# Weights ahead of later activations at the start, a different order in the first row tile, and a bank and an add moved

## The chip, the cores and the metric

The program runs on one core of one Trainium2 chip. The metric is device time in microseconds (us), of which the time before the change was 933.08 us in the median of its first three runs. Beside the device time each run lists its *span*, from the first to the last instruction of the core. The span is 1.7 to 3.5 us shorter than the device time and scatters less, so where a few tenths matter I compare spans. I also use the mean granted clock of TensorE that each run lists.

## The reference, cut to what matters

```python
xn = layernorm(x)                                     # x: 2048 x 640
s  = attention(xn, k_cache, v_cache, wq) @ wo         # 32 heads, window of 512 keys
g  = silu((silu(xn @ w_gate) * (xn @ w_up)) @ w_down) # w_gate, w_up: 640 x 1536
out = x + s * g
```

The kernel does the feed-forward part first, 512 rows at a time in four blocks, and then attention over pairs of heads. The change touches only the first 20 us (loads, layer norm and the first gate and up products) and the last 10 us (the final multiply and add of the last row tiles).

## The kernel before: what the change and the argument touch

Loads. A load has a queue, SP's or ACT's, and the order of issue on a queue is the order below. `load_gu(q)` brings one quarter of the columns of `w_gate` and of `w_up`, 480 KB each.

```python
def load_x(t):                              # one row tile: 128 rows of x, 160 KB
    ...
    if t < 2:
        for r, eng in ((lo, nc.sync), (hi, nc.scalar)):    # half on each queue
            eng.dma_start(out=x_t[t][r, :], ...)
    else:
        nc.sync.dma_start(out=x_t[t][:], ...)
...
for t in range(4):
    load_x(t)
load_gu(0, nc.scalar)                       # w_gate on SP's queue, w_up on ACT's
load_gu(1)
```

The first block goes row tile by row tile, because its rows arrive that way. For every row tile the layer norm takes statistics and a normalization on VectorE (and a square root on ACT), five transposes on TensorE into the PSUM tile `tp`, and a copy of `tp` to `xnT`, on ACT (`ready`; for row tile 0 VectorE takes two of the five chunks). `first[f]` are PSUM tiles for the first three chunks of 128 hidden columns; index 0 is gate and 1 is up. `keep_warm(n)` issues n dummy matmuls on zeros.

```python
first = {f: [sc[:, s, :] for s in range(2)] for f, sc in ((0, sc_tile()), (1, sc_tile()))}
first[2] = [mm[:, s, :] for mm in (mm_tile(),) for s in range(2)]
tp = psum.tile([P, 2, 1024], bf, name="tp", tag="mm")     # two buffers with tag "mm"
...
ln_stats(1, lambda: ln_apply(0))       # tile 0's normalization between the halves of tile 1's statistics
ready(0)
keep_warm(2)
for t in range(4):
    for f in range(3):
        if f == 2 and t < 3:
            if t < 2:
                ln_stats(t + 2, lambda: ln_apply(t + 1))
            else:
                ln_apply(t + 1)
            ready(t + 1)
        for s in range(2):             # gate, then up, of the same chunk
            hidden_mm(first[f][s][:, rows], s, f, rows)   # a group: 5 matmuls of 128 columns
        if t == 3:
            hidden_gate(0, f, *first[f])                  # Silu on ACT, then multiply on VectorE
...
def ffn_hidden(b, f):                  # every later chunk, 512 columns at once
    gu = sc_tile()
```

At the end, for each of the last row tiles, VectorE multiplies the projection in PSUM by `g2` (`s_f`) and then VectorE (`V`) or POOL (`G`) adds the accumulated sum (`ob`). The very last tile is done in two halves, both on VectorE.

```python
for qt in range(4):
    store(2)
    wo_last(3, qt, G if qt else V)
```

The softmax here doesn't subtract the row's maximum and nothing guards it: scores larger than these inputs give would overflow.

## Time and profile before

| | before |
|---|---|
| device time, median of the first 3 runs | 933.08 us |
| span of the profiled run | 931.3 us |
| TensorE busy | 99% |
| first gate matmul of row tile 0 | 8.83 us |
| first 512-column matmul (fourth chunk) | 19.23 us |
| last matmul's end to the end of the span | 5.34 us |

The two points in time in the middle of the table split the kernel into three stretches. The first is the wait for data, the second is the four row tiles of the first block, and all of the rest is one stretch in which TensorE hardly ever stops.

From the page of the kernel before: the first line of the part on busy time, and the shares by engine of the chain of work that ended last.

```profile
PE 921.0 (99%) x8008; PEld 580.2 (62%) x8024; DVE 579.9 (62%) x845; ACT 476.2 (51%) x849; POOL 66.6 (7%) x58
...
PE 98%; DMA 1%; DVE 1%; ACT 0%; SPq 0%; issue 0%; DVEq 0%
```

TensorE (PE) is the limit. Only 10.3 us of the span lie outside its work, and nearly all of that is at the two ends.

The timeline of the kernel before, at its start. Columns: start in us, duration in us, engine, line, operation, output and inputs, count, and in brackets how long the engine had been idle and for what.

```profile
3.34 1.00 SPq L190 DMA_DIRECT2D wg_sb<-in_B_w_gate_dram  x2
...
6.19 0.59 PE L213 MATMUL sc<-zero_t 128*128 128x512 bf16 x2
...
6.90 0.29 DVE L321 COPY xnT<-tp 128x256 bf16<-128x256 bf16 x1 [0.75 <-ACT xnT L319]
...
8.83 0.45 PE L269 MATMUL sc<-xnT,wg_sb 128*128 128x128 bf16 x5 [2.04 <-DMA wg_sb<-in_B_w_gate_dram]
...
9.46 0.74 PE L269 MATMUL sc<-xnT,wg_sb 128*128 128x128 bf16 x5
...
14.76 0.44 PE L269 MATMUL sc<-xnT,wg_sb 128*128 128x128 bf16 x5 [0.22 <-ACT xnT L319]
...
19.23 1.24 PE L269 MATMUL sc<-xnT,wg_sb 128*128 128x512 bf16 x4 [0.30 <-DVE hT L277]
```

The normalized row tile 0 is in `xnT` at 7.19 us, but the weights are not there: issued fifth on the queue, at 3.34, they let TensorE start at 8.83. Then a group of five matmuls takes 0.74 us where it takes 0.44 later (0.53 against 0.28 from one group's start to the next). Two more waits follow, for ACT's copy and, before the fourth chunk, for VectorE to release a PSUM buffer.

The same kernel by windows of one microsecond. The last three columns are the granted clock, the DMA share and GB/s.

```profile
core 0: us, PE busy (x) PEld busy (x) DVE busy (x) ACT busy (x) POOL busy (x), PEclk, DMA share, GB/s
...
8.00:9.00 1.00, 0.17 (x3) 0.17 (x4) 0.96 (x4) 0.00 (x0) 0.00 (x0) 1.00 1.10 329
9.00:10.00 1.00, 1.00 (x16) 1.00 (x14) 0.14 (x1) 0.00 (x0) 0.00 (x0) 0.66 1.10 325
10.00:11.00 1.00, 1.00 (x12) 1.00 (x11) 0.00 (x0) 0.00 (x0) 0.00 (x0) 0.50 1.10 328
...
13.00:14.00 1.00, 1.00 (x22) 1.00 (x20) 0.48 (x2) 0.00 (x0) 0.00 (x0) 1.00 1.11 333
```

TensorE is "1.00 busy" at 10 us and at 13 us, yet it completes 12 matmuls in the one and 22 in the other. The granted clock is the reason: by the trace's records it is half from 9.32 to 12.74 us. (The records begin at 5.91 us, with the first full-speed mark. Before that mark the PEclk column shows 1.00 because nothing is recorded; the 512-column dummies there follow each other at 0.43 us, against 0.216 later.)

The timeline of the kernel before, at its end.

```profile
924.12 3.04 POOL L541 TENSOR_TENSOR ob<-s_f,sacc 128x640 bf16<-128x640 f32 x2 [3.09 <-DVE s_f L538]
...
925.40 0.57 PE L495 MATMUL mm<-wo_p,OT_b 128*128 128x320 bf16 x3
...
925.72 1.78 DVE L536 TENSOR_TENSOR ob<-s_f,sacc 128x320 bf16<-128x320 f32 x1
927.43 0.48 DVE L535 TENSOR_TENSOR s_f<-mm,g_76 128x320 f32<-128x320 f32 x1
927.94 0.49 DVE L536 TENSOR_TENSOR ob<-s_f,sacc 128x320 bf16<-128x320 f32 x1
```

VectorE's add of half a tile takes 1.78 us at 925.72 and 0.49 us at 927.94. The long one runs while POOL adds two tiles of its own, until 927.16.

### The profile page before, as it was taken

To read this page: it belongs to the slowest core of one execution; us is meant where nothing else is said; L and a number is where in the kernel's file an instruction comes from. 1 tells how busy PE (TensorE), PEld (TensorE's weight loads), DVE (VectorE), ACT (ScalarE), POOL (GpSimd) and SP (SyncE) were. 2 spreads that over 40 slices of the span, in tenths; PEclk is the share of its full clock that TensorE was granted. 3 is DMA by queue.
4 is the path that set the end of the run, shared out by engine and by line. 5 is a ranking of instruction groups with operands and counts; after the bars stand their busy time and mean duration, and the time that the engine had idled before them with its cause. 6 is when DMAs were issued, how large, how long until landed. Compare 5 with 4: busy or idle time off the path is not lost.

```text
span 931.3 us, 18790 instructions
## 1 busy us (share of the span) xinstructions
PE 921.0 (99%) x8008; PEld 580.2 (62%) x8024; DVE 579.9 (62%) x845; ACT 476.2 (51%) x849; POOL 66.6 (7%) x58
## 2 busy tenths in 40 slices
PE   8999999999999999999999999999999999999997
PEld 5455556574757575757575757565666666666675
DVE  5433321377676767676766767676767676767656
ACT  3222222566565655555555555555555555656561
POOL 0000000000000000000000000000000000003976
PEclk9999999999999999999999999999999999999999
DMA  9312510044434434343434252525262616162523
GB/s 297 71 27 61 113 24 11 1 78 86 81 83 74 89 71 91 72 92 67 97 60 104 55 108 53 110 48 116 41 122 35 128 35 128 35 139 64 146 60 107
DMA packets 240100, 76.34 MB, mean 82 GB/s; under 512 B 221072, under 2 KB 240016, under 8 KB 240016
## 3 DMA queue, kind: packets, MB, share of 16 engines
q1 hardware_dynamic: 239200, 74.48, 37.8%
q8 instruction: 63, 1.03, 0.5%
q10 hardware_dynamic: 816, 0.66, 0.3%
q14 instruction: 21, 0.17, 0.1%
HBM read 39.45 MB, written 2.62 MB: 45 GB/s over the span
## 4 chain that ended last, share of the span: by engine, by line
PE 98%; DMA 1%; DVE 1%; ACT 0%; SPq 0%; issue 0%; DVEq 0%
PE sc L495 22%; PE mm L412 22%; PE mm L448 18%; PE sc L426 18%; PE sc L269 11%; PE mm L291 6%; PE sc L448 1%; DMA wg_sb<-in_B_w_gate_dram 1%; PE mm L304 0%; DVE ob L536 0%; SPq L184 0%; ACT xnT L319 0%; PE mm L426 0%; ACT L325 0%; PE mm L269 0%
## 5 line engine op out<-in xcount | busy, mean ns | idle before, releaser
L430 ACT ACTIVATE p_t<-sc 128x1024 bf16<-128x1024 f32 x254 | 253.1, 1023 | 136.4 <-PE sc L426 136.4
L417 DVE TENSOR_REDUCE qT<-mm 128x512 bf16<-128x1024 f32 x189 | 231.3, 1224 | 104.0 <-PE mm L412 101.6
L465 ACT ACTIVATE O_b<-mm,r 128x192 bf16<-128x192 f32 x484 | 164.5, 422 | 175.2 <-DVE r L454 96.5
L412 PE MATMUL mm<-xnT,wq_p 64*128 64x512 bf16 x1890 | 235.0, 376 | 0.0
L495 PE MATMUL sc<-wo_p,OT_b 128*128 128x320 bf16 x1482 | 223.4, 299 | 0.0
L510 DVE TENSOR_TENSOR sacc<-sacc,sc 128x640 f32<-128x640 f32 x216 | 176.7, 821 | 60.9 <-PE sc L495 60.9
L426 PE MATMUL sc<-qT,khat 64*128 64x512 bf16 x1524 | 195.5, 376 | 0.0
L448 PE MATMUL mm<-V_p,p_t 128*128 128x193 bf16 x1984 | 185.8, 246 | 0.0
L448 PEld LDWEIGHTS <-p_t 128*128 128x128 bf16 x2048 | 173.0, 97 | 14.9 <-issue 7.0
L495 PEld LDWEIGHTS <-OT_b 128*128 128x128 bf16 x1488 | 143.5, 98 | 47.3
L412 PEld LDWEIGHTS <-wq_p 64*128 64x128 bf16 x1890 | 90.7, 94 | 112.4 <-issue 4.2
L426 PEld LDWEIGHTS <-khat 64*128 64x128 bf16 x1536 | 74.7, 94 | 91.0
L277 DVE TENSOR_TENSOR hT<-sc,sg 128x512 bf16<-128x512 f32 x47 | 32.4, 690 | 86.2 <-ACT sg L276 86.2
L513 POOL TENSOR_TENSOR sacc<-sacc,g_76 128x640 f32<-128x640 f32 x16 | 22.1, 1402 | 757.8 <-ACT O_b L465 757.8
L454 DVE RECIPROCAL r<-mm 128x4 f32<-128x4 f32 x124 | 22.7, 183 | 73.1 <-PE mm L448 68.9
L276 ACT ACTIVATE sg<-sc 128x512 bf16<-128x512 f32 x47 | 28.0, 597 | 75.2 <-PE sc L269 72.1
L269 PE MATMUL sc<-xnT,wg_sb 128*128 128x512 bf16 (+1 forms) x252 | 59.4, 357 | 3.5 <-DMA wg_sb<-in_B_w_gate_dram 2.0
L269 PE MATMUL sc<-xnT,wu_sb 128*128 128x512 bf16 (+1 forms) x264 | 59.8, 357 | 0.1
L291 PE MATMUL mm<-wd_sb,hT 128*128 128x320 bf16 x384 | 56.6, 299 | 0.0
L291 PEld LDWEIGHTS <-hT 128*128 128x128 bf16 x384 | 37.6, 98 | 18.9
L269 PEld LDWEIGHTS <-wg_sb 128*128 128x128 bf16 x285 | 26.7, 101 | 26.3 <-DMA wg_sb<-in_B_w_gate_dram 2.5
L269 PEld LDWEIGHTS <-wu_sb 128*128 128x128 bf16 x285 | 26.5, 100 | 26.5
(63 smaller groups left out, 249.1 us busy)
## 6 DMA issues: line engine op xcount, KB each, us to landing
wo_p<-in_A_wo_dram SPq DMA_DIRECT2D x16, 480.0 KB, 4.3
K_p<-in_A_k_cache_dram SPq DMA_DIRECT2D x32, 192.0 KB, 3.4
V_p<-in_A_v_cache_dram SPq DMA_DIRECT2D x32, 192.0 KB, 3.1
wq_p<-in_A_wq_dram SPq DMA_DIRECT2D x64, 80.0 KB, 3.1
wq_p<-in_A_wq_dram SPq DMA_DIRECT2D x16, 160.0 KB, 3.2
x_r<-in_A_x_dram SPq DMA_DIRECT2D x16, 160.0 KB, 3.6
x_t<-in_A_x_dram SPq DMA_DIRECT2D x14, 160.0 KB, 3.0
wg_sb<-in_B_w_gate_dram SPq DMA_DIRECT2D x4, 480.0 KB, 6.6
```

The costliest lines, as they stand in the source:

```text
L269: nc.tensor.matmul(out, w_sb[:, c, f * P : (f + 1) * P], xnT[:, c, qc], start=(c == 0), stop=(c == NC - 1),)
L276: nc.scalar.activation(sg[:], g, ACT.Silu)
L277: nc.vector.tensor_tensor(hTs[b][:, f, :], u, sg[:], ALU.mult)
L291: nc.tensor.matmul(dn[:, 0:HD], hTs[b][:, f, ti * P : (ti + 1) * P], wd_sb[:, f, cols], start=(f == 0), stop=(f == NF - 1),)
L412: nc.tensor.matmul(q_ps[:, h, :], pairs[pr]["wq"][r, c, j * P : (j + 1) * P], xnT[r, c, b * 512 : (b + 1) * 512], start=(c == 0), stop=(c ...
L417: nc.vector.reduce_sum(qTs[i][:, j, :], q_ps[:, :, :].rearrange("p h n -> p n h"), axis=AX.X)
L426: nc.tensor.matmul(sc[:, h, :], khat[r, j, ks], qT[r, j, :], start=(j == 0), stop=(j == 2))
L430: nc.scalar.activation(p_t[:, :, :], sc[:, :, :], ACT.Exp, scale=scale)
L448: nc.tensor.matmul(acc[:, k, h * 256 : h * 256 + Dh + 1], Ps[i][kc][:, h, qt * P : (qt + 1) * P], V_p[:, kc, h, 0 : Dh + 1], start=(kc == ...
L465: nc.scalar.activation(O_b[:, qt, h, :], a_k[:, h, 0:Dh], ACT.Copy, scale=r[:, k, h, :])
L495: nc.tensor.matmul(ps, OTs[i][:, 3 * qt + j, :], pairs[i // NB]["wo"][:, j, n * HD : (n + 1) * HD], start=(first and j == 0), stop=(end an ...
L510: nc.vector.tensor_tensor(s_t, s_t, sc[:, :, 0:HD], ALU.add)
```

## The change

Its intent: bring the first weight quarter before row tiles 2 and 3 of x, since row tile 0 needs it first; let row tile 0 do all gate groups before the up groups, since `w_gate` lands ahead of `w_up`; fill the shorter wait with four dummies; put the fourth chunk into the buffer of the transposes, which is free early; and let POOL add only one of the last tiles.

```diff
         def load_x(t, eng=nc.sync):
-            if t < 2:
+            if t == 0:
                 for r, eng in ((lo, nc.sync), (hi, nc.scalar)):
...
-        for t in range(4):
-            load_x(t)
+        load_x(0)
+        load_x(1, nc.scalar)
         load_gu(0, nc.scalar)
+        load_x(2)
+        load_x(3)
         load_gu(1)
...
-            gu = sc_tile()
+            gu = mm_tile() if (b, f) == (0, 3) else sc_tile()
...
+        tp = psum.tile([P, 2, 1024], bf, name="tp", tag="mm")
         first[2] = [mm[:, s, :] for mm in (mm_tile(),) for s in range(2)]
-        tp = psum.tile([P, 2, 1024], bf, name="tp", tag="mm")
...
-        keep_warm(2)
+        keep_warm(4)
         for t in range(4):
-            for f in range(3):
-                if f == 2 and t < 3:
+            order = [(f, s) for s in range(2) for f in range(3)]
+            for k, (f, s) in enumerate(order if t == 0 else sorted(order)):
+                if k == 4 and t < 3:
                     ...                          # statistics, normalization, transposes of tile t+1
-                for s in range(2):
-                    hidden_mm(first[f][s][:, rows], s, f, rows)
+                hidden_mm(first[f][s][:, rows], s, f, rows)
...
-        wo_last(3, qt, G if qt else V)
+        wo_last(3, qt, V if qt else G)
```

More of the change, by code (lines that the diff above doesn't have):

```diff
@@ L178, with load_x @@
         x_t, ln, xns = {}, {}, {}
-        def load_x(t):
+        def load_x(t, eng=nc.sync):
             x_t[t] = lnx.tile([P, D], bf, name="x_t")
-            if t < 2:
+            if t == 0:
                 for r, eng in ((lo, nc.sync), (hi, nc.scalar)):
@@ L185, in load_x @@
             else:
-                nc.sync.dma_start(out=x_t[t][:], in_=x2[t * P : (t + 1) * P, :])
+                eng.dma_start(out=x_t[t][:], in_=x2[t * P : (t + 1) * P, :])
         def load_gu(q, eng=nc.sync):
@@ L340 @@
                     ready(t + 1)
-                for s in range(2):
-                    hidden_mm(first[f][s][:, rows], s, f, rows)
-                if t == 3:
+                hidden_mm(first[f][s][:, rows], s, f, rows)
+                if t == 3 and s == 1:
                     hidden_gate(0, f, *first[f])
```

## The prediction

> What bounds it. TensorE is busy 99% of the 931.3 us span and is 98% of the chain that ended last (page). Of the 10.3 us without a matmul, 5.3 us are the tail after the last one (ends 925.97) and about 4.0 us lie in the first 19.3 us (timeline), so only edges can gain. The middle has DMA far from full and is not touched. The change edits both edges.
>
> Start, before (timeline, chain of waits). xnT of row tile 0 is ready at 7.19 us, but w_gate's first quarter, fifth on the SP queue (issued 3.34), lands 5.44 us later; TensorE idles 2.04 us, to 8.83. Then the granted clock is 0.5 from about 9.3 to 12.6 (windows: 0.66, 0.50, 0.50, 0.63): five 128-column matmuls take 0.53 us instead of 0.28. That costs about 3.3 x 0.5 = 1.65 us. I read it as the Trainium skill, "TensorE: Matmul & The Clock Gate", Part 1: a free-running activity window of about 3.4 us gates the clock to half after too little work; the 3.3 us here agree. Row tiles 2 and 3 wait 0.22 us each for ACT's xnT copy, and the fourth chunk waits 0.30 us for VectorE to free its bank (at 19.23).
>
> Start, after.
> - w_gate's quarter is issued second on SP, about 1.4 instead of 3.34. Bytes ahead of its end are about 1.1 MB less; with the slow first 2 us of the queues I estimate landing at 6.9 to 7.3, w_up's at 7.2 to 7.7 (6.8 before).
> - x tile 1 goes whole to ACT's queue, landing about 4.2, no later than before: VectorE's order (stats of tile 1, then apply of tile 0) doesn't slip. x tile 2 slips from before 7.1 to about 7.5, so xn of tile 1 comes about 8.5 instead of 8.14.
> - Gate columns first need w_up 0.56 us later than before. Four warming matmuls (4 x 0.22) end at 7.05, so no idle window.
> - Row tile 0 starts at 7.1 to 7.4 (minus 1.5 us). Clock stays full (minus 1.65). Because the work is faster, tile 1 now waits for ACT's copy and xn, 0.3 to 0.7 us (plus 0.5). Tiles 2 and 3 follow at the 2.34 us period seen before.
> - Fourth chunk in the transposes' bank: minus 0.30.
> Sum: first 512-column matmul at about 16.3 instead of 19.23: minus 2.9. Everything later is TensorE-bound and shifts with it.
>
> Tail. Before, the last half tile's VectorE add takes 1.78 us instead of 0.49, because POOL adds the two tiles before it until 927.2 (Trainium skill, "SBUF — State Buffer", SBUF: two separate sides: a GpSimd op and a VectorE op with two SBUF inputs exclude each other; the add ends 0.34 us after POOL, which agrees). After, POOL adds only the first tile (about 922.5 to 924.05), VectorE the next two, 0.82 each. Adding VectorE's queue from 922.8: first add held until 924.05, ends 924.72, then 0.82+0.82+0.48+0.49+0.43+0.49 gives 928.3, against 928.43. The contention becomes queueing: about minus 0.1.
>
> Predicted: 933.1 - 2.9 - 0.1 = 930.1; I take 930.3 for DMA luck. Range 929.4 to 931.8. Within 2%: 98%.
>
> What would show it: first gate matmul at about 7.2; PEclk full from 6 us on; no wait for VectorE before the fourth chunk; first 512-column matmul near 16.3; last matmul to end of span still about 5.2 us; VectorE adds of the last tiles 0.82, 0.49 instead of 1.78.
>
> What would make it wrong: the two weight quarters contending so that gate lands after 8; x tile 2 landing after 8, holding tile 1; the clock window falling otherwise in either kernel (run-to-run about 1.2 us in the before times); x tile 1 landing after 4.4, delaying tile 0.

## The result

| | before | after |
|---|---|---|
| device time, median (6 runs each) | 933.22 us | 931.0 us |
| span of the profiled run | 931.3 | 928.8 |
| first gate matmul of row tile 0 | 8.83 | 7.66 |
| first 512-column matmul | 19.23 | 17.05 |
| from the one to the other | 10.40 | 9.39 |
| last matmul's end to the end of the span | 5.34 | 5.04 |

The ratio of the times is 0.9976, with a 95% interval of 0.9963 to 0.9989. It is the mean time of the changed kernel's fast runs over the mean of the other's fast runs of the same rounds, so it is not quite the ratio of the medians. The change gains 2.2 us of device time, where I predicted 2.8 (933.1 to 930.3).

The page of the changed kernel, the same two lines.

```profile
PE 920.7 (99%) x8026; PEld 578.7 (62%) x8026; DVE 579.7 (62%) x846; ACT 476.2 (51%) x849; POOL 65.1 (7%) x57
...
PE 98%; DMA 1%; DVE 1%; ACT 0%; issue 0%; SPq 0%; DVEq 0%
```

Nothing is to be seen at this scale: a gain of 2.2 us in 931 does not show in shares. The start, in the timeline of the changed kernel:

```profile
1.38 0.80 SPq L190 DMA_DIRECT2D wg_sb<-in_B_w_gate_dram  x1
...
6.05 1.03 PE L215 MATMUL sc<-zero_t 128*128 128x512 bf16 x4
...
7.66 0.73 PE L271 MATMUL sc<-xnT,wg_sb 128*128 128x128 bf16 x10 [0.58 <-DMA wg_sb<-in_B_w_gate_dram]
...
8.37 0.49 DVE L225 BATCH_NORM_STATS2 stats<-x_t 128x6 f32<-128x320 bf16 x1 [1.32 <-DMA x_t<-in_A_x_dram]
...
8.96 0.45 DVE L248 TENSOR_SCALAR xn<-x_t,mv,rstd 128x640 bf16<-128x640 bf16 x1
...
9.47 0.45 PE L259 MATMUL tp<-ident,xn 128*128 128x128 bf16 x5 [0.52 <-DVE xn L248]
...
10.70 0.44 PE L271 MATMUL sc<-xnT,wg_sb 128*128 128x128 bf16 x5 [0.22 <-ACT xnT L321]
...
17.05 1.24 PE L271 MATMUL mm<-xnT,wg_sb 128*128 128x512 bf16 x5
```

The weights come earlier and TensorE starts 1.17 us sooner. But a new wait has come: VectorE waits 1.32 us for the x of row tile 2, which now lies behind the weights on SP's queue, and the normalization of row tile 1 stands behind it in VectorE's order. The transposes of tile 1 wait for that at 9.47, and row tile 1 starts only at 10.70. The wait before the 512-column matmul is gone.

By windows, the changed kernel:

```profile
9.00:10.00 1.00, 0.53 (x10) 0.54 (x11) 0.96 (x4) 0.04 (x1) 0.00 (x0) 1.00 1.09 328
10.00:11.00 1.00, 0.78 (x15) 0.66 (x13) 0.54 (x3) 0.85 (x2) 0.00 (x0) 1.00 1.11 336
...
13.00:14.00 1.00, 0.96 (x18) 0.96 (x18) 0.61 (x2) 0.98 (x2) 0.00 (x0) 1.00 1.10 330
```

The granted clock stays at 1.00. And the end:

```profile
920.35 1.54 POOL L543 TENSOR_TENSOR ob<-s_f,sacc 128x640 bf16<-128x640 f32 x1 [1.50 <-DVE s_f L540]
...
921.50 1.08 DVE L543 TENSOR_TENSOR ob<-s_f,sacc 128x640 bf16<-128x640 f32 x1
...
923.34 0.83 DVE L543 TENSOR_TENSOR ob<-s_f,sacc 128x640 bf16<-128x640 f32 x1
...
925.53 0.49 DVE L538 TENSOR_TENSOR ob<-s_f,sacc 128x320 bf16<-128x320 f32 x1
```

VectorE's 1.78 us add is gone; one add of a whole tile is still held a little by POOL (1.08 instead of 0.83 us). VectorE ends 2.23 us after the last matmul (923.79), against 2.46 before.

The difference of the two profiled spans, 2.47 us, splits so: 1.17 (start of row tile 0) + 1.01 (row tiles) + 0.29 (the rest). What lies in the 1.01 was the question for the experiments: how much is the clock, how much the bank, and what the new wait takes back.

### The profile page after: what moved, and what is told of

It is laid out like the page before. It is cut to its first block, busy times and chain, and to the rows that moved or that the text cites. A ratio compares the mean times of both kernels' runs of the same rounds, so it can differ in the third digit from the quotient of the medians.

```text
span 928.8 us, 18808 instructions
## 1 busy us (share of the span) xinstructions
PE 920.7 (99%) x8026; PEld 578.7 (62%) x8026; DVE 579.7 (62%) x846; ACT 476.2 (51%) x849; POOL 65.1 (7%) x57
## 4 chain that ended last, share of the span: by engine, by line
PE 98%; DMA 1%; DVE 1%; ACT 0%; issue 0%; SPq 0%; DVEq 0%
PE sc L497 22%; PE mm L414 22%; PE mm L450 18%; PE sc L428 18%; PE sc L271 10%; PE mm L293 6%; DMA x_t<-in_A_x_dram 1%; PE sc L450 1%; PE mm L306 0%; PE mm L271 0%; ACT xnT L321 0%; DVE s_f L540 0%; PE mm L428 0%; ACT L327 0%; DVE ob L538 0%
```

## The experiments

### The wait filled with dummies, nothing else

```diff
-        keep_warm(2)
+        keep_warm(11)          # in the kernel before
```

> The kernel before with one edit: 11 instead of 2 dummy matmuls ahead of row tile 0, so that TensorE has work (9 more x 0.216 us) until about 8.5 us, where w_gate's first quarter lands at 8.8. Theory (an idle window of about 2 us makes the clock fall to half from 9.3 to 12.6 us): the granted clock stays 1.00 after 6 us, row tile 0 still starts at 8.8, and the first 512-column matmul comes about 1.6 us earlier minus one exposed wait for ACT's copy of tile 1 (0.4): at 18.0 instead of 19.23. Time down 1.2 us, and the runs closer together than the 1.9 us of before. Rival (the clock falls for another reason, such as its phase or the start of dense real data): still about 0.5 between 9 and 13 us, first 512-column matmul at 19.2, time the same.

The granted clock stayed at 1.00. The gate weights landed late in this execution (first gate matmul at 9.36), but from there to the first 512-column matmul it took 9.15 us instead of 10.40. The windows of this kernel:

```profile
9.00:10.00 1.00, 0.96 (x14) 0.64 (x13) 0.66 (x3) 0.00 (x0) 0.00 (x0) 1.00 1.10 329
10.00:11.00 1.00, 1.00 (x22) 1.00 (x20) 0.00 (x0) 0.03 (x1) 0.00 (x0) 1.00 1.10 328
```

Twenty-two matmuls between 10 and 11 us, where the kernel before made 12, and a difference of 1.25 us in the row tiles, net of the copy wait that a fall hides. That fits idle time as what takes the clock away, but this one profile does not show it, since the kernel before also has executions without a fall; the shares of all profiles, in the next section, are the evidence. Yet the time did not change: ratio 0.9998 (0.9986 to 1.0011), 932.36 us against 932.32. The expectation of 1.2 us was wrong, and the list of runs shows why. The nine runs of the kernel before in these rounds are of two sorts: three have a span of 931.5 to 931.9 us and a mean clock of 0.997 or 0.998, and six have 929.9 to 930.5 and 0.999 or 1.0. By this, the clock fell at the start in a third of the runs only. I call these bad draws and the others good ones. The dummies' five runs had spans of 930.0 to 930.7, all with a clock of 0.999 or 1.0: they show no bad draw and gain nothing on a good one. (They may cost a little on a good one, since eleven dummies end at about 9.3 us even when the weights land sooner. That is argued, not shown.)

### The kernel before, twice more

> The kernel before once more, unedited, for another profile of its start. Theory (the clock falls only when the phase of the 3.4 us windows puts most of the idle time into one of them, so in some executions and not in others): w_gate lands at 8.8 to 9.5; with a fall the row tiles 0 and 1 take 5.9 us from the first gate matmul to row tile 2, without one 4.7, and the span is 931.5 to 931.9 or 929.9 to 930.5. Rival: always a fall, span 931 or more.

> The same as the run above, another draw: a fall and 5.9 us, or none and 4.7 us.

Both draws came. The first has no fall: first gate matmul at 8.72, first 512-column matmul at 17.87, which is 9.15 us, and a span of 930.0.

```profile
8.72 0.45 PE L269 MATMUL sc<-xnT,wg_sb 128*128 128x128 bf16 x5 [1.73 <-DMA wg_sb<-in_B_w_gate_dram]
...
17.87 1.24 PE L269 MATMUL sc<-xnT,wg_sb 128*128 128x512 bf16 x5 [0.29 <-DMA wg_sb<-in_B_w_gate_dram]
```

(The wait in the last bracket is put down to a load, but that quarter had landed by about 10 us; VectorE's first multiplication, from 17.13 to 17.8, is what frees the buffer. The releasers are inferred, and the same wait of 0.29 has VectorE as its releaser in the next fence.) The second has a fall, from 10.6 us on: 9.50, then 19.90, which is 10.40 us, and a span of 932.0.

```profile
9.50 0.45 PE L269 MATMUL sc<-xnT,wg_sb 128*128 128x128 bf16 x5 [2.10 <-DMA wg_sb<-in_B_w_gate_dram]
...
19.90 0.81 PE L269 MATMUL sc<-xnT,wg_sb 128*128 128x512 bf16 x3 [0.29 <-DVE hT L277]
```

So the same program takes 9.15 or 10.40 us for the same work, as the clock has it. Over the three sets of rounds the kernel before was run 27 times: 17 runs with spans of 931.2 to 933.0 us and a mean clock of 0.998 or less, 10 with 929.9 to 930.5 and 0.999 or more. (The sets ran on three chips: 3 of 9 runs fell on the first, 7 of 9 on each of the others. The good draws agree across chips, with means of 930.2 to 930.4, so spans can be compared between sets when like draws are.) The profile that I predicted from is of the first sort too. (The mean clock alone is not enough: it also counts the last few microseconds of the span, when TensorE has stopped and the clock can fall again, so a run without a fall at the start can show 0.998, as the profiled one of "the normalization of tile 1 ahead" below does. The two sorts are 0.7 us apart in span.)

When does it fall? The trace records the changes of the clock, and they lie on a grid of windows of 3.41 us. In each of the 14 profiles I took the share of the window after the first full-speed mark in which TensorE was busy. The four profiles with a fall had 34, 38, 39 and 40%. The ten without had 48, 49, 57 and more. The windows at the end of the span, where TensorE stops, agree and narrow it: one with 43% was not followed by a half clock, three with 37 to 38% were. The windows are found from the records; that the share of one window decides is inferred from these figures.

What differs between executions is two things. The first is the length of the gap, which the landing of `w_gate` ends: in the first of the two above it is 1.73 us, and wherever a window of 3.41 us is laid over that trace, TensorE has at least 49%, so by these figures it would not have fallen at any phase. In the four that fell it was 2.04 to 2.24 us. That also fits the spans: a bad draw is 1.6 us longer than a good one on average, 0.3 more than the fall itself costs. The second is the phase of the windows relative to the program (the first mark lies between 4.6 and 7.2 us). In the five profiles with this load order and two dummies the gap lay whole in one window. The one profile in which a window's edge cut it in two is the next one. So how much of the draw is phase and how much landing is not shown.

### The load order alone

```diff
-        for t in range(4):
-            load_x(t)
+        load_x(0)
+        load_x(1, nc.scalar)
         load_gu(0, nc.scalar)
+        load_x(2)
+        load_x(3)              # in the kernel before; row order, dummies, banks and tail as before
```

> The kernel before with the new load order alone (w_gate and w_up ahead of x tiles 2 and 3, x tile 1 whole on ACT's queue); row order, 2 dummies, banks and tail as before. Theory: w_gate lands at 7.6, w_up at 8.3, x tile 2 at 8.35 as in the profile after, so row tile 0 starts at 7.65, waits about 0.4 for w_up, and row tile 1 is held by x tile 2 (its stats stand ahead of the normalization of tile 1 on VectorE) and starts at 10.7 as after. If the clock stays full: first 512-column matmul at 17.5 (17.05 plus the bank wait), minus 1.7 us; if the idle time (about 1.2 + 0.4 + 0.6 us) makes the clock fall, at 18.5 to 19. This tells what the gate-first row order and the two more dummies add to the load order: theory nothing but the safety of the clock.

The gate weights landed only at 8.85 in the profiled execution, and the x of tile 2 at 9.64 (expected 7.6 and 8.35): the landing of one and the same load order varies by more than a microsecond. In the trace's records of DMA packets one of the 16 engines finished its part of `w_up` at 8.83 us, the other 15 by 7.26; a load has landed when the slowest has. The row tiles took 9.90 us, which is the 9.15 of a full clock, plus 0.28 for `w_up` between the first gate and the first up group, plus 0.46 for the x of tile 2. The clock did not fall (48% busy in the window), by luck of the phase: the gap of 2.37 us was cut at 8.15, and a window that held it whole would have had 26%. The five spans were 929.3 to 931.2, mean 930.16: no better than a good draw of the kernel before, 930.2. By itself the load order is meant to bring the weights sooner; in this profile they landed no sooner (8.85 against 8.79), and it adds the two waits. By their clock at most one of the five runs can have fallen (one shows 0.998, the others more), against three of nine of the kernel before; that is too few to show that bad draws get rarer. The time is not resolved from before (ratio 0.9996, 0.9983 to 1.0008).

### The bank alone, and the tail alone

```diff
+        tp = psum.tile([P, 2, 1024], bf, name="tp", tag="mm")
         first[2] = [mm[:, s, :] for mm in (mm_tile(),) for s in range(2)]
-        tp = psum.tile([P, 2, 1024], bf, name="tp", tag="mm")
...
-            gu = sc_tile()
+            gu = mm_tile() if (b, f) == (0, 3) else sc_tile()
```

> The kernel before with the bank swap alone (transposes' bank taken first, fourth chunk in that bank). Theory: the 0.30 us wait for VectorE before the fourth chunk goes, first 512-column matmul about 0.45 us after the same point of row tile 3 (2.13 us from tile 3's first matmul to it becomes 1.67); nothing before it moves: start of row tile 0 at 8.8, the half clock from about 9.3 on again (a second look at whether the clock falls in another execution). Rival: the wait only moves to the fifth chunk, whose bank is freed by the same VectorE multiplication; then no gain at the sixth chunk. Time down 0.3 to 0.5 us, inside the noise of this kernel.

```profile
9.15 0.45 PE L269 MATMUL sc<-xnT,wg_sb 128*128 128x128 bf16 x5 [2.24 <-DMA wg_sb<-in_B_w_gate_dram]
...
19.09 1.24 PE L269 MATMUL mm<-xnT,wg_sb 128*128 128x512 bf16 x4
```

The clock fell here, and the row tiles took 9.94 us where 10.40 is the figure with a fall: 0.46 less. The stretch from the first 512-column matmul to the end of the span was 912.09 us, against 912.08 in the kernel before, so the wait did not move to the sixth chunk. (In the timeline that wait reads 0.30; from one group's start to the next it is 0.46, because the idle time is counted only from the modelled end of the last matmul.) The times don't resolve it: 1.0006, 0.9993 to 1.0018. By their spans (930.9 to 931.5) and a clock of 0.998 all five runs fell, against three of nine of the kernel before beside them; why so many is not known. Bad draw against bad draw, the mean span is 931.2 against 931.7, which agrees with the 0.46.

```diff
-        wo_last(3, qt, G if qt else V)
+        wo_last(3, qt, V if qt else G)     # in the kernel before
```

> The kernel before with the last row tiles' adds swapped alone (first on POOL, next two on VectorE). Theory from the two profiles: end of the last matmul to the end of the span falls from 5.33 to about 5.0 us, VectorE's last add 2.23 us after the last matmul's end instead of 2.46, since VectorE's own queue is then the limit; time down 0.2 to 0.3 us. Rival (my prediction): minus 0.1 or nothing. The start is that of before, with a half clock from about 9.3 us if the clock falls in every execution.

```profile
923.18 1.54 POOL L541 TENSOR_TENSOR ob<-s_f,sacc 128x640 bf16<-128x640 f32 x1 [1.50 <-DVE s_f L538]
...
928.36 0.49 DVE L536 TENSOR_TENSOR ob<-s_f,sacc 128x320 bf16<-128x320 f32 x1
```

From the last matmul's end to the end of the span it took 5.11 us, where the kernel before took 5.33 to 5.35 in its three profiles; VectorE ended 2.23 us after the last matmul. The gain is 0.22 to 0.24 us, more than my 0.1, and far below the 1.3 us by which the one add had been stretched: what POOL no longer holds up, VectorE now has to do itself. The times (1.0001, 0.9987 to 1.0014) do not resolve 0.2 us; by their spans three of the five runs fell.

### The changed kernel with the old order in row tile 0

```diff
-            for k, (f, s) in enumerate(order if t == 0 else sorted(order)):
+            for k, (f, s) in enumerate(sorted(order)):        # in the changed kernel
```

> The changed kernel with the row order of before in row tile 0 (gate and up alternating). Theory (row tile 1 is held by x tile 2, so time lost in tile 0 on w_up comes out of a later wait): row tile 0 waits 0.3 to 0.5 us for w_up's quarter after its first gate group, row tile 1 still starts at 10.7 plus or minus the luck of the landings, first 512-column matmul at 17.0, span the same as after within 0.3. Rival (the gate-first order earns what it was meant to): 0.4 us later.

The weights landed at 8.2 and the x of tile 2 at 9.0, a bad draw, but from the first gate to the first 512-column matmul it took 9.48 us, as in the two profiles of the changed kernel (9.39 and 9.49). The five spans were 928.6 to 929.5, mean 928.9; the changed kernel's eleven had a mean of 929.1. The gate-first order earns nothing here, because row tile 1 waits for the x of tile 2 either way.

### The changed kernel without its dummies

```diff
-        keep_warm(4)               # in the changed kernel
```

> The changed kernel without its 4 dummy matmuls before row tile 0. Theory: nothing of the time is theirs as such; TensorE idles from about 6.2 to 7.65 instead of from 7.05, and the clock only falls if a window of 3.4 us has less than about 40 to 49% work (40, 38 and 34% in the three profiles that fell, 49% in the one with the new loads that did not). Expect 50 to 56% here: no fall in the profile, row tile 1 at 10.7, first 512-column matmul at 17.0, spans 929 like after, with one or two of the runs about 1.3 us longer with a mean clock of 0.998 or less. Rival (the four dummies are what keeps the clock): a fall in most runs, spans 930.3 or more.

The profile had no fall (57% busy in its window), row tile 1 at 10.68, the first 512-column matmul at 17.02 and a span of 928.8, as in the changed kernel. Four of the five runs had 928.7 to 929.1; one had 930.6, with a clock of 0.998. The dummies have no worth of their own, but without them a bad draw seems to happen; with them none of eleven runs has such a span (two show a clock of 0.998, with 929.1 and 929.3 like the rest). One run in five is thin evidence. The traces say more: wherever a window of 3.41 us is laid over the start of the changed kernel, TensorE has at least 67% in one profile and 80% in the other; without the dummies the least is 44%, close to the 40% of a fall.

### The normalization of tile 1 ahead of the statistics of tile 2

```diff
-                    if t < 2:
+                    if t == 0:                 # in the changed kernel
+                        ln_apply(1)
+                        ln_stats(2)
+                    elif t < 2:
                         ln_stats(t + 2, lambda: ln_apply(t + 1))
```

> The changed kernel with one edit: on VectorE the normalization of row tile 1 stands ahead of the statistics of tile 2, instead of between their halves. Theory (in the profile after, row tile 1 is held because tile 2's x lands at 8.35 us behind w_gate's quarter, and VectorE waits for it 1.32 us with the normalization of tile 1 behind it): xn of tile 1 at about 7.7, transposed at 8.8 after the fourth group instead of 9.47, row tile 1 starts at 10.0 instead of 10.7, first 512-column matmul at 16.4 instead of 17.05; span down about 0.7 us from the 929.1 mean of after. Rival (row tile 1 is held by something else: ACT's copy, w_up, TensorE's own work): row tile 1 within 0.2 us of 10.7, span the same.

Row tile 1 started at 9.88, the first 512-column matmul at 16.23. The lines of this kernel's timeline:

```profile
7.59 0.45 DVE L248 TENSOR_SCALAR xn<-x_t,mv,rstd 128x640 bf16<-128x640 bf16 x1
...
8.66 0.44 PE L259 MATMUL tp<-ident,xn 128*128 128x128 bf16 x5
...
9.88 0.44 PE L271 MATMUL sc<-xnT,wg_sb 128*128 128x128 bf16 x5 [0.22 <-ACT xnT L321]
```

The normalization now runs at 7.59 instead of 8.96, and the transposes follow the fourth group without a wait. Row tile 0 started at 7.54, so the row tiles took 8.69 us instead of 9.39 to 9.49: 0.7 to 0.8 us, as the theory has it. Four of the five spans were 927.8 to 928.0, one was 929.3; the device time was 929.72 us, ratio to before 0.9964 (0.995 to 0.9978). So the new wait was the x of tile 2, through VectorE's order. (The 929.3 has a clock of 1.0, so it is no fall.)

### The x of tile 2 on ACT's queue, w_up behind w_gate on SP's

```diff
         load_x(1, nc.scalar)
-        load_gu(0, nc.scalar)
-        load_x(2)
+        load_x(2, nc.scalar)           # in the changed kernel
+        load_gu(0)
         load_x(3)
```

> The changed kernel with one edit: x tile 2 goes to ACT's queue behind tile 1, and w_up's quarter to SP's queue behind w_gate's. Theory (w_gate's quarter lands at 7.6, later than the 6.9 to 7.3 that I predicted, because w_up's quarter shares the 16 engines with it from the other queue; and x tile 2 waits behind both): w_gate lands at about 6.7, w_up at 7.8, x tile 2 before 6; row tile 0 starts at 7.1, tile 1 at 9.5, first 512-column matmul at 15.9 instead of 17.05; span down 1.1 us. Rival (the slow first packets of a queue and single late engines set the landing, not the sharing): w_gate still lands after 7.3; row tile 1 still gains the 0.7 us of x tile 2.

The last part of `w_gate` was written at 6.25 us by the trace's packet records, and TensorE started at 7.04, with no wait for it; in the changed kernel's first profile it had waited for `w_gate` until 7.66. The x of tile 2 was written by 5.73; `w_up` released its first group at 8.11, which shows as 0.2 us lost.

```profile
7.04 0.74 PE L271 MATMUL sc<-xnT,wg_sb 128*128 128x128 bf16 x10
...
8.11 0.45 PE L271 MATMUL sc<-xnT,wu_sb 128*128 128x128 bf16 x5
...
9.62 0.44 PE L271 MATMUL sc<-xnT,wg_sb 128*128 128x128 bf16 x5 [0.22 <-ACT xnT L321]
```

The first 512-column matmul came at 15.96, the five spans were 927.7 to 928.2, and the device time 929.83 us, ratio 0.9961 (0.9949 to 0.9974). In the six profiles with `w_up` on the other queue `w_gate` landed at 7.20 to 8.85 us; with `w_up` behind it, at 6.59 here and at 7.16 in the next experiment. So sharing the engines with the other queue is the likely cause of its delay, but with two profiles, and landings that vary as much, it is not proven. The Trainium skill, "DMA: Bandwidth & Descriptors", section "Issuing engines are not separate DMA queues", says the same: DMAs started by different engines run on the same 16 DMA engines and interleave. This run agrees, with the 0.6 us by which TensorE starts sooner than in the changed kernel's first profile.

### The two together, and less wait for the copy

```diff
         load_x(1, nc.scalar)
-        load_gu(0, nc.scalar)
-        load_x(2)
+        load_x(2, nc.scalar)                       # in the changed kernel
+        load_gu(0)
...
-            if t == 2:
+            if t == 3:
                 nc.scalar.activation(act_t[:], one_t[:], ACT.Silu)    # loads ACT's table
...
-                if k == 4 and t < 3:
-                    if t < 2:
+                if k == 3 and t < 3:
+                    if t == 0:
+                        ln_apply(1)
+                        ln_stats(2)
+                    elif t < 2:
```

> The changed kernel with x tile 2 on ACT's queue, w_up's quarter behind w_gate's on SP's, the normalization of tile 1 ahead of the statistics of tile 2, the next tile's transposes after 3 of a tile's 6 groups instead of 4, and ACT's table for Silu loaded after the last xnT copy instead of before it. Theory (what remains of waits in the profile with x tile 2 on ACT's queue is 0.4 us in front of each of tiles 1, 2 and 3 for ACT's copy of xnT, which three groups, 0.84 us, nearly cover, and 0.2 us for w_up): row tile 0 at 7.1, tile 1 at 9.1, tile 2 at 11.2, tile 3 at 13.3, first 512-column matmul at 15.0; span 926.8, against 927.9 of the two better single edits and 929.1 of after. Rival (xn of the next tile comes too late for the earlier transposes, so the wait only changes its name): first 512-column matmul at 15.7 or later, span 927.6.

```profile
8.70 0.73 PE L271 MATMUL sc<-xnT,wu_sb 128*128 128x128 bf16 x10 [0.21 <-DMA wu_sb<-in_B_w_up_dram]
...
9.55 0.44 PE L271 MATMUL sc<-xnT,wg_sb 128*128 128x128 bf16 x5
...
11.61 0.44 PE L271 MATMUL sc<-xnT,wg_sb 128*128 128x128 bf16 x5
...
15.39 1.24 PE L271 MATMUL mm<-xnT,wg_sb 128*128 128x512 bf16 x5
```

Row tiles 1 and 2 now start without a wait of note, and the row tiles take 8.19 us in all. The spans were 926.6 to 927.6, mean 927.1, against 926.8 expected; in the profile `w_up` was late (it landed at 8.65 instead of the 8.1 of the run before). The parts of this edit were not all tried apart. The device time is 929.05 us, ratio to before 0.9953 (0.9939 to 0.9966), with correct results. It is better than the changed kernel, run again beside it:

> The changed kernel once more, unedited, for a second profile and for times beside the version above. Expect w_gate's quarter to land between 7.5 and 8.3 (as in the other profiles with this load order: 7.5 to 8.9), first 512-column matmul at 17.0 to 17.7, spans 928.6 to 929.6, no fall of the clock before the end.

The repeat gave 930.68 us, spans of 928.6 to 930.0, first gate at 7.49, first 512-column matmul at 16.98, tail 5.04, and no fall.

## Why the prediction was right or wrong

The predicted time, 930.3 us in a range of 929.4 to 931.8, holds the measured 931.0, and the chance given to "within 2%" was right. The sum behind it was larger than the real one by about 0.7 us in the first 512-column matmul ("at about 16.3 instead of 19.23: minus 2.9"; measured 17.05, so minus 2.2): 0.33 from the start of row tile 0 and 0.57 from the new waits, less 0.16 by which the bank was worth more. The tail made up another 0.2. So the errors offset each other in part, and that is luck. Term by term:

- **"Row tile 0 starts at 7.1 to 7.4 (minus 1.5 us)."** It started at 7.66 and, in the repeat, 7.49; minus 1.2 to 1.3. The mis-sized term is the landing of `w_gate`, "6.9 to 7.3". I had `w_up` on the other queue in my count, but let `w_gate` finish ahead of it. With `w_up` queued behind instead, TensorE started at 7.04 without waiting for `w_gate`. In the repeat the weights were not even the limit: `w_gate` had landed at 7.39, but the four dummies, which stand behind transposes that had still run at the low clock, were not done, and the first gate matmul follows the last of them at 7.49 without a pause.
- **"x tile 2 slips from before 7.1 to about 7.5, so xn of tile 1 comes about 8.5."** The mechanism was right, and named as a danger ("x tile 2 landing after 8, holding tile 1"), but the size was wrong: it landed at 8.35, and xn came at 9.41. I had written "tile 1 now waits for ACT's copy and xn, 0.3 to 0.7 us (plus 0.5)". Measured, from one group's start to the next, it is 0.69 for xn and 0.38 for the copy, 1.07 together. This is the largest error of the sum; the two experiments that take the x of tile 2 out of the way gain 1.0 to 1.2 us of the mean span (the second also by its earlier start).
- **"Clock stays full (minus 1.65)."** In the executions where the clock falls this is right: 1.63 us, of which the exposed copy wait takes 0.38 again. But it is not a property of the kernel. By spans and clock it fell in 17 of 27 runs of the kernel before and in none of 11 of the changed one. Set against a good draw of before (span 930.2), the change gains 1.1 us; against a bad one (931.8), 2.7. The prediction named the clock's luck among what would make it wrong ("the clock window falling otherwise in either kernel") and yet counted the fall in full.
- **"Fourth chunk in the transposes' bank: minus 0.30."** Minus 0.46, shown alone.
- **Tail, "about minus 0.1".** Minus 0.3. The form of the argument held ("The contention becomes queueing"): the Trainium skill, "SBUF — State Buffer", section "SBUF: two separate sides", says that the port pair shared by VectorE and GpSimd is held exclusively for a whole instruction, and the adds of 1.78, 1.08 and 0.49 us agree. VectorE's end came 0.23 us sooner, where my sum of its queue gave 0.13; the other 0.07 came after VectorE's end, and the run with the tail alone does not have it.
- **"Gate columns first need w_up 0.56 us later" and "Four warming matmuls (4 x 0.22) end at 7.05, so no idle window."** Both true of the trace, and both nearly worthless: the old row order costs nothing, and without the dummies four of five runs were the same. Where `w_gate` comes early the dummies even stand in its way, as in the repeat.

The terms close. From the first gate to the first 512-column matmul, before took 10.40 us; taking 1.63 for the clock and 0.46 for the bank and adding 0.69 and 0.38 of waits gives 9.38, and the profile shows 9.39.

What stays open: why the start of row tile 0 varies by 1.4 us with one load order (first gate at 7.5 to 8.9 in six profiles with the new order), beyond the fact that single DMA engines finish late; how far the phase and how far the landing decides the draw; and exactly where between 40 and 43% of activity the clock falls.

## What to carry to other kernels

When you move a load forward, ask what it pushes back, and follow that through the order of the engine that consumes it: here a tile that nobody needed yet held up the normalization of one that everybody waited for, only because its statistics stood ahead in VectorE's program. Before costing a half clock that you see in one profile, look at the clock and span of every run: if they come in two groups, it is a draw, and the change is worth its share of bad draws plus what it gains on a good one. Shortening idle stretches at the start pays on every draw, and again where it averts a fall; filling them with dummy work pays only on the bad draws.

## What the Trainium skill lacked or had wrong

- "TensorE: Matmul & The Clock Gate", Part 1, has the clock return to half after at least one idle window of about 3.4 us, and its rule is to avoid idle gaps longer than that. Here gaps of 2.0 to 2.2 us were enough: windows of 3.41 us with 34, 38, 39 and 40% of TensorE activity were followed by a half-clock window, windows with 43 (at the end of a span), 48, 49 and 57% were not. The length of the window and its free phase agree.
- The same page puts the cost at throttled time times one minus the clock ratio. That nearly held for the work (it gives 1.71 us for the 3.41 at half clock; 1.63 measured), but a fall also hid a wait of 0.38 us, so the net was 1.25 us. The page says that the number of slow matmuls at the start varies between runs of a kernel, but not that a later fall can come in some runs of a program and not in others; here it was 17 of 27.
- "DMA: Bandwidth & Descriptors" has no figure for how much the landing of the same loads varies between executions: at the start of this kernel the first quarter of `w_gate` landed between 7.20 and 8.85 us with one load order, and in one trace a single engine of 16 finished 1.6 us after the others.
